# A two-pass channel-attention kernel: first-pass loads in sizes that fall from 44 to 3 rows, and the maxima kept in two halves that take turns

## The chip, the cores and the metric

The kernel runs on one core of one Trainium2 chip. The metric is the device time of one execution in microseconds (us), less is better. Before the change it was 743.05 us (median of 3 runs, 742.87 to 743.95). A "row" in this text is a slice of the input that puts 384 bf16 channels on each of 128 partitions, 98,304 bytes.

## The reference

```python
def reference(x, w1, w2):            # x (1,384,384,384) bf16, w1 (384,96), w2 (96,384)
    xf = x.reshape(B, H * W, C)
    gap = jnp.mean(xf, 1)            # mean over 147,456 pixels, per channel
    gmp = jnp.amax(xf, 1)            # maximum over them
    h_a = relu(gap @ w1)             # (written there as h * (h > 0))
    h_m = relu(gmp @ w1)
    scale = sigmoid(h_a @ w2 + h_m @ w2)
    return x * scale[:, None, None, :]
```

Every output depends on all of x, so x (113.2 MB, 1152 rows) must be read once for the statistics and multiplied afterwards. What stays on chip need not be read again.

## The kernel before

Six slots of 44 rows in SBUF take turns as buffers. In the first pass TensorE adds up each load (sums over partitions with a vector of ones) and VectorE folds it into `acc`, a running maximum over 11 rows. The last 6 x 44 rows stay in the slots, 18 more in PSUM; the other rows are read again in the second pass, where VectorE multiplies slot by slot in place and the ACT queue stores. Between the passes lies the **turn**: `acc` is folded from 11 rows to one, transposed, put through the two small matrices and the sigmoid. No store can start before that, and there is nearly no free memory to load into.

```python
LAST_LOADS = ((22, 22),) * 9 + (      # how the last 14 blocks of 44 rows are cut into loads
    (11, 11, 11, 11), (17, 16, 11), (11, 11, 11, 11), (11, 11, 11, 11), (10, 9, 9, 8, 8),
)
SUM_TAIL = 2                          # loads whose sums take a shorter path at the end
...
for i, (first, n, s, lo, hi) in enumerate(loads):
    rows = slots[s][:, lo:hi, :]
    m = hi - lo
    ...nc.sync.dma_start(out=rows[:, a:b, :], in_=...)
    ...sums(rows, m, ...) or tail_sums(rows, m, ...)            # TensorE
    for j in range(0 if i else A, m, A):                        # A = 11
        k = min(A, m - j)
        nc.vector.tensor_tensor(out=acc[:, 0:k, :], in0=acc[:, 0:k, :], in1=rows[:, j:j + k, :], op=ALU.max)
...
n = A                                                           # the fold: 11 -> 6 -> 3 -> 2 -> 1 rows
while n > 1:
    h = n // 2
    nc.vector.tensor_tensor(out=acc[:, 0:h, :], in0=acc[:, 0:h, :], in1=acc[:, n - h:n, :], op=ALU.max)
    n -= h
    ...                                                         # freed rows of acc are read in again
```

## Time and profile before

| what | value | view |
|---|---|---|
| span of the profiled execution | 741.5 us | page |
| read from HBM, written | 198.92 MB, 113.25 MB | page |
| mean rate | 421 GB/s | page |
| VectorE (DVE) busy | 66% of the span, over 90% in most of the first pass | page |
| fold starts, first multiply | 271.43 us, 276.93 us | chain |

The page cuts the span into 40 slices of 18.5 us. A digit is the busy share in tenths; the last line is what the DMA engines moved:

```profile
DVE  6789999999999989999444443444444444444600
DMA  9999999999999969999999999999999999999997
GB/s 383 423 435 434 433 430 418 428 429 426 427 422 422 418 254 378 402 435 446 432 431 428 432 437 436 436 432 432 427 434 437 436 436 432 432 427 432 441 437 340
```

The DMA engines are full in every slice but the fifteenth, the turn, where they move 254 GB/s (and the last, where the work runs out). VectorE is nearly full from the fourth slice to the fourteenth, but that does not make it the bound: it has about as much work as the loads give it time for.

The table of stretches gives the turn more closely. The columns are the stretch and its length, then busy time and count for TensorE, weight loads, DVE, ACT and POOL, the granted clock, the DMA share and GB/s:

```profile
260.00:270.00 10.00, 6.76 (x75) 3.77 (x70) 9.83 (x6) 0.95 (x4) 0.00 (x0) 0.50 0.81 331
270.00:280.00 10.00, 2.28 (x30) 1.48 (x27) 7.88 (x13) 0.83 (x3) 0.00 (x0) 0.50 0.59 177
280.00:290.00 10.00, 0.00 (x0) 0.00 (x0) 10.00 (x8) 0.00 (x0) 0.00 (x0) 0.50 0.99 396
```

Lost DMA time here is 10 x (1 - 0.81) + 10 x (1 - 0.59), about 6 us. (A packet is counted in the stretch in which it starts, so a share can come out a little over 1.)

TensorE waits for every load in the first pass, so its timeline shows when loads land. The columns are start, busy time, engine, line, operation, and in brackets the idle time before and what ended it:

```profile
25.44 4.06 PE L143 MATMUL bank_a<-x_84,small 128*1 128x512 bf16 x33 [7.40 <-DMA x_84<-in_x_dram]
35.46 4.17 PE L143 MATMUL bank_a<-x_79,small 128*1 128x512 bf16 x33 [5.96 <-DMA x_79<-in_x_dram]
46.95 4.86 PE L143 MATMUL bank_a<-x_80,small 128*1 128x512 bf16 x33 [7.32 <-DMA x_80<-in_x_dram]
...
256.64 1.34 PE L143 MATMUL bank_a<-x_83,small 128*1 128x512 bf16 x9 [1.22 <-DMA x_83<-in_x_dram]
259.22 1.34 PE L143 MATMUL bank_a<-x_83,small 128*1 128x512 bf16 x9 [1.24 <-DMA x_83<-in_x_dram]
```

A 44-row load lands every 10.02 us (35.46 from 25.44), an 11-row load every 2.58 us (259.22 from 256.64; 2.57 on average). The step from 35.46 to 46.95 is 1.5 us too long. From the two sizes, (10.02 - 2.57) / 33 rows makes 0.226 us of DMA time per row. Four loads of 11 rows take about 0.26 us longer than one of 44, which is 0.08 to 0.09 us for each further transfer; the prediction works with 0.083.

The groups by form, those of one slot, give VectorE's cost of a maximum over 11, 10 and 8 rows (4224, 3840 and 3072 elements per partition; busy us and mean ns of one are after the bar, then idle time before them):

```profile
L183 DVE TENSOR_TENSOR acc<-acc,x_84 128x4224 bf16<-128x4224 bf16 x16 | 37.7, 2358 | 5.2 <-DMA x_84<-in_x_dram 4.7
L183 DVE TENSOR_TENSOR acc<-acc,x_84 128x3840 bf16<-128x3840 bf16 x1 | 2.2, 2159 | 0.0
L183 DVE TENSOR_TENSOR acc<-acc,x_84 128x3072 bf16<-128x3072 bf16 x2 | 3.5, 1758 | 0.1
```

Last, the chain of work that ended last, around the turn (start, duration, what):

```profile
267.84 1.77 DVE acc L183
269.61 0.02 issue
269.64 1.77 DVE acc L183
271.40 0.02 issue
271.43 1.17 DVE acc L203
...
276.93 1.50 DVE x_79 L226 x3
```

The maximum of the last 8 rows (269.64 to 271.41) is the last thing before the fold at 271.43. From there to the first multiply it is 5.5 us.

### The profile page before, as it was taken

What the parts mean: (1) busy time and instruction counts of PE and PEld (TensorE: products, weight loads), DVE (VectorE), ACT (ScalarE), POOL (GpSimd) and SP (SyncE); (2) the same over time, 40 slices, a digit from 0 to 9 for tenths busy, and PEclk for the clock granted to TensorE, in tenths of its full rate; (3) what the DMA queues carried; (4) which work ended last, traced back from release to release, by engine and by line L of the source; (5) the groups of instructions that cost most, each with busy time, mean ns of one, the idle gap of its engine ahead of it and who ended that gap; (6) DMA issues with size and microseconds to landing.
All of it is one profiled execution on the core that took longest, in us unless ns stands there. A gap on an engine that the chain in (4) does not pass through costs nothing.

```text
span 741.5 us, 2477 instructions
## 1 busy us (share of the span) xinstructions
PE 127.2 (17%) x966; PEld 40.6 (5%) x966; DVE 489.4 (66%) x168; ACT 3.3 (0%) x9; POOL 0.7 (0%) x6
## 2 busy tenths in 40 slices
PE   3345443445454550000000000000000000000000
PEld 0011111111111120000000000000000000000000
DVE  6789999999999989999444443444444444444600
ACT  0000000000000000000000000000000000000000
POOL 0000000000000000000000000000000000000000
PEclk9865666655555555555555555555555555555555
DMA  9999999999999969999999999999999999999997
GB/s 383 423 435 434 433 430 418 428 429 426 427 422 422 418 254 378 402 435 446 432 431 428 432 437 436 436 432 432 427 434 437 436 436 432 432 427 432 441 437 340
DMA packets 18379, 312.32 MB, mean 421 GB/s; under 512 B 2400, under 2 KB 3008, under 8 KB 6592
## 3 DMA queue, kind: packets, MB, share of 16 engines
q1 hardware_dynamic: 12032, 198.92, 63.2%
q10 hardware_dynamic: 6336, 113.25, 35.7%
q8 instruction: 7, 0.11, 0.1%
q14 instruction: 4, 0.03, 0.0%
HBM read 198.92 MB, written 113.25 MB: 421 GB/s over the span
## 4 chain that ended last, share of the span: by engine, by line
another core or an unknown queue 44%; DMA 34%; DVE 14%; DVEq 1%; SPq 1%; issue 1%; PE 0%; ACT 0%; ACTq 0%
DMA x_81<-in_x_dram 9%; DMA x_82<-in_x_dram 7%; DVE acc L183 7%; DMA out_dram<-x_83 6%; DMA x_79<-in_x_dram 6%; DMA x_80<-in_x_dram 3%; DMA x_83<-in_x_dram 3%; DVE x_81 L226 1%; DVE x_80 L226 1%; DVE x_83 L226 1%; DVE x_82 L226 1%; DVE x_79 L226 1%; DVEq L313 1%; SPq L253 1%
## 5 line engine op out<-in xcount | busy, mean ns | idle before, releaser
L226 DVE TENSOR_TENSOR x_79<-x_79,scale_bc 128x16896 bf16<-128x16896 bf16 (+6 forms) x13 | 45.4, 3538 | 34.2 <-DMA x_79<-in_x_dram 33.0
L226 DVE TENSOR_TENSOR x_80<-x_80,scale_bc 128x16896 bf16<-128x16896 bf16 (+4 forms) x9 | 40.9, 4576 | 28.7 <-DMA x_80<-in_x_dram 28.7
L226 DVE TENSOR_TENSOR x_84<-x_84,scale_bc 128x16896 bf16<-128x16896 bf16 x4 | 35.8, 8958 | 33.1 <-DMA x_84<-in_x_dram 33.1
L226 DVE TENSOR_TENSOR x_83<-x_83,scale_bc 128x16896 bf16<-128x16896 bf16 x4 | 35.8, 8956 | 33.0 <-DMA x_83<-in_x_dram 33.0
L226 DVE TENSOR_TENSOR x_82<-x_82,scale_bc 128x16896 bf16<-128x16896 bf16 x4 | 35.8, 8957 | 32.8 <-DMA x_82<-in_x_dram 32.8
L226 DVE TENSOR_TENSOR x_81<-x_81,scale_bc 128x16896 bf16<-128x16896 bf16 (+3 forms) x6 | 36.0, 6021 | 31.0 <-DMA x_81<-in_x_dram 31.0
L183 DVE TENSOR_TENSOR acc<-acc,x_84 128x4224 bf16<-128x4224 bf16 (+3 forms) x21 | 47.3, 2253 | 5.4 <-DMA x_84<-in_x_dram 4.7
L143 PEld LDWEIGHTS <-small 128*1 128x1 bf16 x900 | 36.4, 110 | 229.9 <-issue 227.0
L183 DVE TENSOR_TENSOR acc<-acc,x_83 128x4224 bf16<-128x4224 bf16 (+1 forms) x19 | 42.8, 2253 | 1.3 <-DMA x_83<-in_x_dram 0.7
L183 DVE TENSOR_TENSOR acc<-acc,x_80 128x4224 bf16<-128x4224 bf16 (+1 forms) x18 | 40.6, 2257 | 3.0 <-DMA x_80<-in_x_dram 2.4
L183 DVE TENSOR_TENSOR acc<-acc,x_79 128x4224 bf16<-128x4224 bf16 (+1 forms) x17 | 38.9, 2287 | 1.5 <-DMA x_79<-in_x_dram 1.0
L183 DVE TENSOR_TENSOR acc<-acc,x_81 128x4224 bf16<-128x4224 bf16 (+2 forms) x17 | 37.9, 2229 | 1.5 <-DMA x_81<-in_x_dram 1.0
L183 DVE TENSOR_TENSOR acc<-acc,x_82 128x4224 bf16<-128x4224 bf16 x16 | 37.7, 2358 | 1.5 <-DMA x_82<-in_x_dram 1.0
L143 PE MATMUL bank_a<-x_84,small 128*1 128x512 bf16 (+2 forms) x165 | 21.6, 558 | 27.1 <-DMA x_84<-in_x_dram 27.1
L143 PE MATMUL bank_a<-x_79,small 128*1 128x512 bf16 (+1 forms) x150 | 20.4, 574 | 28.7 <-DMA x_79<-in_x_dram 28.7
L143 PE MATMUL bank_a<-x_80,small 128*1 128x512 bf16 (+3 forms) x150 | 21.0, 585 | 23.6 <-DMA x_80<-in_x_dram 23.6
L143 PE MATMUL bank_a<-x_83,small 128*1 128x512 bf16 (+2 forms) x159 | 20.3, 540 | 23.3 <-DMA x_83<-in_x_dram 23.3
L143 PE MATMUL bank_a<-x_82,small 128*1 128x512 bf16 (+2 forms) x138 | 19.6, 594 | 20.9 <-DMA x_82<-in_x_dram 20.9
L143 PE MATMUL bank_a<-x_81,small 128*1 128x512 bf16 (+3 forms) x138 | 19.4, 593 | 21.1 <-DMA x_81<-in_x_dram 21.1
L179 DVE COPY acc<-x_79 128x4224 bf16<-128x4224 bf16 x1 | 1.3, 1260 | 5.4 <-DMA x_79<-in_x_dram 5.4
L185 DVE COPY kept_ps<-x_79 128x3072 uint32<-128x3072 uint32 x1 | 3.4, 3354 | 0.0
L226 DVE TENSOR_TENSOR x_81<-kept_ps,scale_bc 128x6144 bf16<-128x6144 bf16 x1 | 3.4, 3350 | 0.0
(39 smaller groups left out, 22.5 us busy)
## 6 DMA issues: line engine op xcount, KB each, us to landing
x_84<-in_x_dram SPq DMA_DIRECT2D x5, 4224.0 KB, 27.4
x_79<-in_x_dram SPq DMA_DIRECT2D x5, 4224.0 KB, 27.4
x_80<-in_x_dram SPq DMA_DIRECT2D x5, 4224.0 KB, 27.7
x_81<-in_x_dram SPq DMA_DIRECT2D x5, 4224.0 KB, 27.4
x_82<-in_x_dram SPq DMA_DIRECT2D x5, 4224.0 KB, 27.4
x_83<-in_x_dram SPq DMA_DIRECT2D x4, 4224.0 KB, 27.4
out_dram<-x_82 ACTq DMA_DIRECT2D x4, 4224.0 KB, 74.3
out_dram<-x_83 ACTq DMA_DIRECT2D x4, 4224.0 KB, 71.1
```

The source lines that it names most:

```text
L143: nc.tensor.matmul(sum_ps[q * QP:q * QP + 1, 0:g * P], lhsT=ones_bf[:, 0:1], rhs=rows[:, k:k + g, q * P:(q + 1) * P], start=(done + k == 0 ...
L179: nc.vector.tensor_copy(out=acc, in_=rows[:, 0:A, :])
L183: nc.vector.tensor_tensor(out=acc[:, 0:k, :], in0=acc[:, 0:k, :], in1=rows[:, j:j + k, :], op=ALU.max)
L185: nc.vector.tensor_copy(out=kept_ps.bitcast(U32), in_=rows.bitcast(U32))
L226: nc.vector.tensor_tensor(out=dst, in0=src, in1=scale_bc.unsqueeze(1).to_broadcast([P, n, C]), op=ALU.mult)
L253: nc.sync.dma_start(out=slots[s][:, j:j + m, :], in_=rows_of(xr, first, n)[:, j:j + m, :])
L313: with _tile.TileContext(nc) as tc:
```

## The change

The intent is to leave less work behind the last byte: the last load has 3 rows instead of 8, and sizes fall, by and large, all the way (within most staying slots they fall once more), so that VectorE, which is only a little faster than the DMA engines, is done with one load when the next lands. Small loads mean small maxima, and each maximum over `acc` used to wait for the one before. So `acc` is used as two halves of 6 and 5 rows in turn, and an operation depends on the one two back.

```diff
+ACC_PARTS = ((0, 6), (6, 11))
-LAST_LOADS = ((22, 22),) * 9 + (
-    (11, 11, 11, 11), (17, 16, 11), (11, 11, 11, 11), (11, 11, 11, 11), (10, 9, 9, 8, 8),
+PASSING = (
+    43, 44, 44, 43, 43, 44, 43, 42, 42, 39, 38, 37, 36, 36, 35, 34, 32, 29, 29, 27, 27, 23, 21, 15, 13,
+)
+STAYING = (
+    (19, 17, 8), (18, 16, 10), (16, 14, 14), (13, 11, 11, 9), (10, 9, 9, 8, 8), (6, 6, 5, 5, 5, 4, 4, 3, 3, 3),
 )
-SUM_TAIL = 2
+SUM_TAIL = 4
...                                   # (building the list of loads from these; the same rows stay and are re-read)
-        for j in range(0 if i else A, m, A):
-            k = min(A, m - j)
-            nc.vector.tensor_tensor(out=acc[:, 0:k, :], in0=acc[:, 0:k, :], in1=rows[:, j:j + k, :], op=ALU.max)
+        j = 0 if i else A
+        while j < m:
+            c, e = ACC_PARTS[turn]
+            turn = (turn + 1) % len(ACC_PARTS)
+            e = min(e, c + m - j)
+            nc.vector.tensor_tensor(
+                out=acc[:, c:e, :], in0=acc[:, c:e, :], in1=rows[:, j:j + e - c, :], op=ALU.max
+            )
+            j += e - c
```

PASSING are the loads of rows that are read again later, STAYING those of the six slots that stay.

More of the change, by code (lines that the diff above doesn't have):

```diff
@@ L71 @@
     head = PSUM_ROWS + beside
-    left = TOT - head
-    blocks = []
-    slot = NS - 1
-    while left > 0:
-        n = min(SLOTS[slot], left)
-        blocks.insert(0, [left - n + head, n, slot])
-        left -= n
-        slot = (slot - 1) % NS
-    n_blocks = len(blocks)
-    n_stream = n_blocks - NS
+    n_stay = sum(SLOTS)
+    n_pass = TOT - head - n_stay
+    assert sum(PASSING) == n_pass
+    stay = []
+    for i, n in enumerate(SLOTS):
+        stay.append([head + n_pass + sum(SLOTS[:i]), n, i])
+    again = [(head, n_pass % SLOTS[0])] + [
+        (head + n_pass % SLOTS[0] + SLOTS[0] * i, SLOTS[0]) for i in range(n_pass // SLOTS[0])
+    ]
     small = consts.tile([P, 16], BF16)
@@ L128 @@
     loads = [(0, PSUM_ROWS, 0, 0, PSUM_ROWS), (PSUM_ROWS, beside, 1, 0, beside)]
-    for i, (first, n, s) in enumerate(blocks):
-        left = n
-        for m in LAST_LOADS[i - n_blocks] if i >= n_blocks - len(LAST_LOADS) else (n,):
-            m = min(m, left)
-            loads.append((first, n, s, n - left, n - left + m))
-            left -= m
-        assert left == 0
+    done = head
+    for i, n in enumerate(PASSING):
+        loads.append((done, n, (i - len(PASSING)) % NS, 0, n))
+        done += n
+    for (first, n, s), pieces in zip(stay, STAYING):
+        assert sum(pieces) == n
+        for j, m in enumerate(pieces):
+            loads.append((first, n, s, sum(pieces[:j]), sum(pieces[:j + 1])))
     n_loads = len(loads)
@@ L163, in tail_sums @@
                 )
-    done = 0
+    done = turn = 0
     for i, (first, n, s, lo, hi) in enumerate(loads):
@@ L254, in get @@
         assert j == 0
-    order = blocks[n_stream:]
-    again = sorted(blocks[:n_stream], key=lambda b: -b[1])
+    order = list(stay)
+    again.sort(key=lambda b: -b[1])
     stores, reads = list(FIRST_STORES), list(FIRST_READS)
@@ L265, in read_into @@
             again.remove(b)
-            b = (b[0], b[1], s)
+            b = (*b, s)
             get(b, reads.pop(0) if reads else (b[1],))
```

## The prediction

> **What bounds the kernel.** Both passes are bound by the DMA engines, not VectorE. The page's slices show DMA at nine tenths or more in every slice but the turn between the passes (254 GB/s); HBM reads 198.92 MB and writes 113.25 MB at a mean 421 GB/s. The change moves no bytes: rows kept on chip and rows re-read stay the same. From the stretch table, DMA idles for about 6 us around the turn (267 to 281 us). That hole is nearly all that the change can win; 2% would be 15 us.
>
> **First pass.** In the timeline TensorE's waits give the landings: a 44-row load every 10.03 us, two of 22 rows every 10.11, four of 11 every 10.27. So a row costs about 0.226 us and each further DMA about 0.083 us (128 packets over 16 engines: about 10 ns per packet; the Trainium skill, "DMA: Bandwidth & Descriptors", Measured, has about 10.5, and the trace agrees). The built programs have 53 first-pass loads before and 56 after: an estimated +0.25 us to the last landing. The six slots and the eight DMA semaphores leave over 6 us of queued loads throughout, so I expect no starvation.
>
> **VectorE.** A maximum over 11 rows takes 2359 ns and starts every 2.39 us, since each waits for the one before. The forms of 3072 and 3840 elements (1758 and 2159 ns) give 0.2 us per row, so a dependent operation has about 190 ns of overhead. Independent multiplies overlap: five on the second staying slot take 9.23 us although their durations sum to 9.56, about 70 ns of overhead each. In the built program each half waits for the operation two back. So 11 rows should cost 2.2 + 2 x 0.07 = 2.34 us: twice the instructions, yet no slower. The halves' worth is that small loads get affordable: one undivided chain needs 0.79 us for 3 rows, against 0.76 between landings.
>
> **The critical part.** Before, the last 8-row load lands at about 269.6 us; its maximum runs 269.64 to 271.4, then fold (2.7 us), transposes, small products, sigmoid, first multiply at 276.9. After, the last load has 3 rows: 0.76 us of maximum behind a landing at about 269.85, so the fold starts at about 270.65. Everything behind it is unchanged. Gain: 1.0 us less behind the last landing, minus 0.25 us of DMA: about 0.75 us. The sums chain (four tail loads, 13 rows instead of 16) stays off the path, ending over 2 us before it is needed. The second pass is the same program shifted. Predicted 742.3 us, 80% range 741.0 to 743.8; faster by over 2% 0.01, within 2% 0.97, slower 0.02.
>
> **What would show it.** Right: maxima of 6 and 5 rows at about 1.36 and 1.16 us but starting 1.27 and 1.07 us apart; a last maximum of 0.76 us that waited for its load; fold 0.5 to 1.2 us earlier; the turn's slice a little fuller, later slices equal. Wrong: VectorE no longer waiting for loads over the last 40 us (it lags), or a last landing over 1 us later.
>
> **What could make it wrong.** Alternating operations may not overlap: then the 3-to-6-row loads leave VectorE behind and the kernel loses about 2 us. About 120 more VectorE instructions mean a few more instruction fetches on the same DMA engines. One 1.5 us landing slip near 44 us, which I cannot explain, may move or vanish. Small descriptors may cost more than 10 ns each.

## The result, and the profile after

The changed kernel took 742.53 us (median of 4 runs, 741.81 to 745.11) against 743.02 (median of 4) before. The ratio is 0.9996 with a 95% interval of 0.9979 to 1.0013. That is inside the predicted range, and by itself it shows no gain: the interval holds both the predicted gain of 0.75 us and zero. The profiled execution was the slowest of the four, 745.11 us.

The slices of the page:

```profile
DVE  5889999999999989998444433434444444433600
DMA  9999999999999979999999999999999999999997
GB/s 381 436 427 432 432 428 431 424 424 438 417 426 420 414 256 376 427 433 433 433 429 435 435 429 433 433 435 435 429 429 429 435 433 436 435 435 427 425 435 310
```

The turn's slice rose from 254 to 256 GB/s only, but the stretches (columns as before) show that the work has moved forward:

```profile
260.00:270.00 10.00, 6.90 (x63) 3.49 (x60) 10.00 (x13) 0.95 (x4) 0.00 (x0) 0.50 0.84 325
270.00:280.00 10.00, 2.44 (x36) 1.64 (x33) 7.88 (x14) 0.83 (x3) 0.00 (x0) 0.50 0.64 194
280.00:290.00 10.00, 0.00 (x0) 0.00 (x0) 10.00 (x9) 0.00 (x0) 0.00 (x0) 0.50 1.02 409
```

From 260 to 270 us the DMA share is 0.84 instead of 0.81, from 270 to 280 it is 0.64 instead of 0.59. By the same sum as before, 10 x (1 - 0.84) + 10 x (1 - 0.64), 5.2 us of DMA time are lost instead of 6.

The groups by form for the halves of 6 and 5 rows (2304 and 1920 elements):

```profile
L190 DVE TENSOR_TENSOR acc<-acc,x 128x2304 bf16<-128x2304 bf16 x95 | 128.5, 1352 | 11.4 <-DMA x<-in_x_dram 11.2
L190 DVE TENSOR_TENSOR acc<-acc,x 128x1920 bf16<-128x1920 bf16 x93 | 106.3, 1151 | 1.4 <-DMA x<-in_x_dram 1.4
```

One operation still takes 1352 and 1151 ns, but they overlap. The timelines of VectorE for one 44-row load show it; first the kernel before, then the changed one:

```profile
47.00 9.54 DVE L183 TENSOR_TENSOR acc<-acc,x_80 128x4224 bf16<-128x4224 bf16 x4 [1.96 <-DMA x_80<-in_x_dram]
```

```profile
29.95 9.44 DVE L190 TENSOR_TENSOR acc<-acc,x 128x2304 bf16<-128x2304 bf16 x8 [0.79 <-DMA x<-in_x_dram]
```

Eight operations in turn take 9.44 us where four in a chain took 9.54. In this load a half of 6 rows starts 1.27 us before the next half, and one of 5 rows 1.07 us.

The chain around the turn:

```profile
267.77 0.68 DVE acc L190
268.65 0.55 DVE acc L190
269.31 0.61 DVE acc L190
269.98 0.76 DVE acc L190
270.75 0.02 issue
270.77 1.17 DVE acc L213
...
276.26 0.83 DVE x L236 x2
```

The fold starts at 270.77 instead of 271.43, and the first multiply at 276.26 instead of 276.93: 0.66 and 0.67 us earlier. The last four maxima start 0.88, 0.66 and 0.67 us apart.

So the turn gained what was forecast, and yet this execution was slower than any of the kernel before in that comparison. Where did it go? The packet records of the trace show two parts. The first 120 MB had moved 0.67 us sooner than in the trace of before (290.30 against 290.97 us after the start of the first load packet), 310 MB at the same moment (731.98 and 731.97), so 0.7 us were lost on the way. The rest was lost at the very end. The DMA share there, in stretches of 1 us, in this execution:

```profile
738.00:739.00 1.00, 0.00 (x0) 0.00 (x0) 0.00 (x0) 0.00 (x0) 0.00 (x0) 0.50 0.30 115
739.00:740.00 1.00, 0.00 (x0) 0.00 (x0) 0.00 (x0) 0.00 (x0) 0.00 (x0) 0.50 0.09 37
740.00:741.00 1.00, 0.00 (x0) 0.00 (x0) 0.00 (x0) 0.00 (x0) 0.00 (x0) 0.50 0.06 25
741.00:742.00 1.00, 0.00 (x0) 0.00 (x0) 0.00 (x0) 0.00 (x0) 0.00 (x0) 0.50 0.06 25
```

A share of 0.06 is one engine of 16 (1/16 = 0.0625). For about 3 us a single engine or two finish the last stores while the others have nothing left. In the second trace of the same program (the first experiment below) the same end is:

```profile
737.00:738.00 1.00, 0.00 (x0) 0.00 (x0) 0.00 (x0) 0.00 (x0) 0.00 (x0) 0.50 0.47 177
738.00:739.00 1.00, 0.00 (x0) 0.00 (x0) 0.00 (x0) 0.00 (x0) 0.00 (x0) 0.50 0.03 11
```

There the engines finish almost together. This end differs from execution to execution, and by more than the gain.

### The profile page after: what moved, and what is told of

Its sections match the earlier page's. It is cut to its first block, busy times and chain, and to the rows that moved or that the text cites. A ratio compares the mean times of both kernels' runs of the same rounds, so it can differ in the third digit from the quotient of the medians.

```text
span 743.3 us, 2595 instructions
## 1 busy us (share of the span) xinstructions
PE 131.4 (18%) x969; PEld 41.7 (6%) x969; DVE 490.1 (66%) x285; ACT 3.3 (0%) x9; POOL 0.7 (0%) x6
## 4 chain that ended last, share of the span: by engine, by line
another core or an unknown queue 40%; DMA 37%; DVE 15%; DVEq 1%; SPq 1%; issue 1%; PE 0%; ACT 0%; ACTq 0%
DMA x<-in_x_dram 31%; DVE acc L190 11%; DMA out_dram<-x 7%; DVE x L236 2%; DVEq L323 1%; SPq L263 1%; DVE kept_ps L195 0%; DVE acc L213 0%; DVE acc L236 0%; DVE acc L183 0%; PE bank_a L230 0%; ACT scale_bc L231 0%; SPq L174 0%; DVE bank_b L197 0%
## 5 line engine op out<-in xcount | busy, mean ns | idle before, releaser
L236 DVE TENSOR_TENSOR x<-x,scale_bc 128x16896 bf16<-128x16896 bf16 (+11 forms) x40 | 229.1, 5769 | 196.4 <-DMA x<-in_x_dram 195.2
L190 DVE TENSOR_TENSOR acc<-acc,x 128x2304 bf16<-128x2304 bf16 (+5 forms) x225 | 245.9, 1166 | 12.8 <-DMA x<-in_x_dram 12.6
L147 PE MATMUL bank_a<-x,small 128*1 128x512 bf16 (+3 forms) x912 | 126.6, 584 | 140.7 <-DMA x<-in_x_dram 140.7
L195 DVE COPY kept_ps<-x 128x3072 uint32<-128x3072 uint32 x1 | 3.4, 3354 | 0.0
L236 DVE TENSOR_TENSOR x<-kept_ps,scale_bc 128x6144 bf16<-128x6144 bf16 x1 | 3.4, 3351 | 0.0
L213 DVE TENSOR_TENSOR acc<-acc 128x384 bf16<-128x384 bf16 (+2 forms) x4 | 2.6, 658 | 0.1
L236 DVE TENSOR_TENSOR acc<-acc,scale_bc 128x1920 bf16<-128x1920 bf16 (+1 forms) x2 | 2.4, 1250 | 0.0
```

The source lines that it names most:

```text
L147: nc.tensor.matmul(sum_ps[q * QP:q * QP + 1, 0:g * P], lhsT=ones_bf[:, 0:1], rhs=rows[:, k:k + g, q * P:(q + 1) * P], start=(done + k == 0 ...
L190: nc.vector.tensor_tensor(out=acc[:, c:e, :], in0=acc[:, c:e, :], in1=rows[:, j:j + e - c, :], op=ALU.max)
L195: nc.vector.tensor_copy(out=kept_ps.bitcast(U32), in_=rows.bitcast(U32))
L236: nc.vector.tensor_tensor(out=dst, in0=src, in1=scale_bc.unsqueeze(1).to_broadcast([P, n, C]), op=ALU.mult)
```

## The experiments

Two numbers are read from every trace. The first is the start of the fold. As executions start up to 0.3 us apart, it is also given from the first landing (marked by the first matmul of the trace). The second is the total over 5 rounds (4 in the first comparison), beside runs of the kernel before on the same chip.

| run | fold, us | from first landing | median, us | before, same rounds | ratio (95%) |
|---|---|---|---|---|---|
| before, first trace | 271.43 | 267.01 | 743.05 | | |
| e1, before again | 271.13 | 266.99 | 743.07 | 742.86 | 1.0003 (0.9989 to 1.0016) |
| changed, first trace | 270.77 | 266.43 | 742.53 | 743.02 | 0.9996 (0.9979 to 1.0013) |
| a1, changed again | 270.45 | 266.24 | 741.24 | 742.25 | 0.9982 (0.9970 to 0.9995) |
| d1, changed a third time | 270.77 | 266.34 | 741.56 | 742.94 | 0.9986 (0.9974 to 0.9999) |
| a2, old sizes, halves | 271.37 | 267.24 | 743.59 | 742.25 | 1.0014 (1.0001 to 1.0026) |
| d3, the same again | 271.65 | 267.32 | 744.22 | 742.94 | 1.0015 (1.0003 to 1.0027) |
| a3, new sizes, one chain | 273.32 | 269.19 | 744.84 | 742.25 | 1.0032 (1.0019 to 1.0044) |
| a4, coarse end | 271.09 | 266.97 | 743.40 | 742.25 | 1.0011 (0.9997 to 1.0024) |
| b1, thrice the loads | 275.90 | 271.59 | 747.54 | 742.50 | 1.0067 (1.0054 to 1.0080) |
| b2, ten more behind | 270.26 | 266.16 | 746.06 | 742.50 | 1.0048 (1.0036 to 1.0060) |
| b3, three more behind | 270.37 | 266.21 | 742.84 | 742.50 | 1.0009 (0.9993 to 1.0024) |
| c1, fewer loads | 270.25 | 266.05 | 742.71 | 742.50 | 1.0006 (0.9991 to 1.0021) |
| d2, fewer loads again | 270.19 | 266.04 | 742.28 | 742.94 | 0.9996 (0.9982 to 1.0009) |

The fold counted from the first landing repeats within 0.03 us for the kernel before (two traces) and within 0.2 us for the changed one (three). The programs of b2 and b3 are the changed kernel up to the fold; with them five traces lie within 0.27 us, so differences of 0.1 to 0.2 us between single traces mean little. The total cannot tell less than about 1 us: the null run e1 has an interval of plus or minus 0.13%. All kernels gave a correct result.

The moment of the last landing can be read too, from the records of the semaphores that the transfers raise (no view above prints them). The fold is then the sum of two parts: when the last rows land, counted from the first matmul, and the time from there to the fold.

| traces | last landing, us | from there to the fold, us |
|---|---|---|
| before, e1 | 265.07, 265.08 | 1.94, 1.90 |
| changed, a1, d1 | 265.54, 265.33, 265.45 | 0.89, 0.91, 0.89 |
| b2, b3 (the same up to the fold) | 265.27, 265.33 | 0.89, 0.88 |
| a2, d3: old sizes, halves | 265.29, 265.37 | 1.96, 1.96 |
| a3: new sizes, one chain | 265.34 | 3.85 |
| a4: coarse end | 265.01 | 1.96 |
| b1: thrice the loads | 270.70 | 0.89 |
| c1, d2: fewer loads | 264.83, 264.81 | 1.22, 1.22 |

In these traces the first maximum over a load never starts less than 0.09 us after the load has landed. One that starts 0.09 or 0.10 us behind therefore waited for its load, and a longer delay means that VectorE came late.

### a1 and d1: the changed kernel again

No edit.

> The changed kernel once more, for a second trace and a tighter interval. My theory (the gain is 1.0 us less work behind the last landing minus 0.25 us of added transfers; the second pass is untouched) expects the fold again at about 270.8 us (270.77 in its first trace, 271.43 before), the first multiply near 276.3, and 742.0 to 742.7 us, 0.3 to 1.0 us under the kernel before of the same rounds; the 2 to 3 us that the first trace lost between 550 and 700 us are chance and should be gone. Rival: the loss late in the second pass belongs to the change, then this trace shows it again and the time is 744 to 745.

> The changed kernel a third time, for pooling. [...] My theory: fold at 270.4 to 270.8 us in this trace too, the first 120 MB moved 0.6 to 1.0 us sooner than before, and the median time 0.3 to 1.3 us under the kernel before of the same rounds. Rival (the first comparison, ratio 0.9996, was the truth and the second, 0.9982, luck): median within 0.3 us of before or above it.

The fold came at 270.45 and 270.77 us. The loss of the first trace did not come back (by the packets it lay on the way to 310 MB and at the end, not between 550 and 700 us as the first text says), and the times were 741.24 and 741.56 us, 1.0 and 1.4 us under the medians of the kernel before. So the rival (the loss belongs to the change) fell, and so did d1's (the first comparison was the truth). The intervals of a1 and d1 hold 0.66 us, the gain at the turn, so the totals do not show more than that; both traces also ended more evenly than those of before. In d1's trace the first 120 MB had moved 0.4 and 0.6 us sooner than in the two traces of before, at or below the low end of what I wrote.

### e1: the kernel before as a null run

No edit.

> The kernel before, submitted as if it were a candidate: a null run, for a second trace of it and for the size of a difference that means nothing. My theory (the 0.7 to 0.9 us at the turn are the change's, the uneven end of the DMA engines is chance): fold at 271.2 to 271.6 us again, the first 120 MB 290.3 to 290.6 us after the first load packet, and a ratio to itself of 0.999 to 1.001. If this trace has the fold at 270.8 or earlier, the gain that I read from one trace of before was chance; if the ratio to itself is 1.001 or more, the 1.0014 of the old sizes with halves means nothing either.

Its fold at 271.13 us is just outside what I wrote, but the trace started earlier: from the first landing it is 266.99 against 267.01. The ratio of the kernel to itself is 1.0003. So the earlier fold of the changed kernel is not chance: 266.99 and 267.01 against 266.43, 266.24 and 266.34, a gain of 0.66 us between the means.

### a2 and d3: the halves alone

```diff
 (the kernel before, its LAST_LOADS and SUM_TAIL)
+ACC_PARTS = ((0, 6), (6, 11))
-for j in range(0 if i else A, m, A): ...            # one chain over 11 rows
+while j < m: c, e = ACC_PARTS[turn] ...             # as in the change
```

> Load sizes of before, maxima in halves of 6 and 5 rows. My theory: the halves alone gain nothing, as the last load still has 8 rows and VectorE was waiting for it before too; fold at 271.4 to 271.6 us, time equal to before within 0.3 us; VectorE only idles more between loads (about 4 us more in the first pass). Rival (VectorE's speed is what the change buys): fold 0.7 us or more earlier than before, time 742.3 or less.

> Old sizes with halves again: its first showing was 743.59 with a fold at 271.37, equal to before's 271.43. If the excess of 0.9 us in the total was only the uneven end of the DMA engines, the median is now within 0.7 us of before; if the halves cost something in the second pass, it is 0.9 us or more over it again.

The fold did not come earlier: 267.24 and 267.32 us from the first landing, 0.2 to 0.3 later than before. All of that is in the last landing, although no transfer was added; I cannot explain it. From there to the fold it is 1.96 us, about as before. So faster maxima alone gain nothing. In total this version is 0.14% slower, twice, about 1 us, where equality within 0.3 us was expected; the fold explains 0.3. The rest I cannot explain: the trace of a2 had moved 310 MB at the same moment as the first trace of before (731.95 and 731.97 us after the start of the first load packet), that of d3 0.6 us later.

### a3: the new sizes alone

```diff
-ACC_PARTS = ((0, 6), (6, 11))
+ACC_PARTS = ((0, 11),)
```

> The new load sizes, maxima over 11 rows in one undivided chain. My theory: a dependent maximum costs about 0.12 us more than one in turn, so VectorE falls behind over the small loads; the fold starts about 2.8 us later than in the changed kernel, at 273.4 to 273.8 us, and the time is about 2.8 us over it, near 745.2. Rival (the sizes alone do it, the halves are decoration): fold at 270.8, time 742.3.

The chain of this kernel at the turn:

```profile
270.95 0.77 DVE acc L190
271.74 0.77 DVE acc L190
272.53 0.77 DVE acc L190
273.32 1.17 DVE acc L213
```

The 3-row maxima start 0.79 us apart here, against 0.66 and 0.67 in the changed kernel: 0.12 us for each operation that waits for the one directly before it. VectorE falls behind: it begins the last slot 2.3 us after that slot's first landing (0.4 in the changed kernel), so most of the delay has built up in the loads before the last slot. The fold comes at 273.32 us, 2.85 us later than in the changed kernel from the first landing (269.19 against 266.34), and the kernel is 0.32% slower than before. The new sizes without the halves are worse than no change.

### a4: the new sizes and halves, but the old end

```diff
-    ..., (10, 9, 9, 8, 8), (6, 6, 5, 5, 5, 4, 4, 3, 3, 3),
+    ..., (10, 9, 9, 8, 8), (10, 9, 9, 8, 8),
-SUM_TAIL = 4
+SUM_TAIL = 2
```

> The changed kernel, but with its last slot loaded as before in 10, 9, 9, 8, 8 rows (two tail loads for the sums, 16 rows). My theory: five loads fewer bring the last landing 0.41 us earlier, but 8 rows of maximum instead of 3 stand behind it (about 1.1 us more), so the fold starts about 0.6 us later than in the changed kernel, at 271.3 to 271.5 us, and the time goes back to that of before, 742.8 to 743.2. Rival (the gain sits in the earlier sizes, 44 to 13 rows): fold at 270.8 or earlier and 742.3 or less.

The fold is back at 266.97 us from the first landing, the value of before. The last landing is 0.4 us earlier than the mean of the changed kernel, and 1.07 us more lie behind it, as computed. So the whole gain at the turn sits in the last slot's sizes. What the finer sizes of the 1108 rows before it are worth is not shown: with the old sizes and halves (a2, d3) VectorE also began the last slot 0.10 us after its first landing, so it came there in time without them. They do need two transfers fewer (46 instead of 48). No run joined the old sizes, the halves and the new last slot. The total, 0.11% over before, is inside what the null run allows. (271.09 us is 0.2 below what I wrote, as this trace started early.)

### b1: what a transfer costs

```diff
+        elif 2 <= i < 2 + len(PASSING):
+            cuts = [0, m // 3, 2 * m // 3, m]       # three transfers for one load, 50 more in all
```

> The changed kernel with each of its 25 passing loads issued as three transfers of a third of the rows: 50 transfers more, same bytes, same maxima. My theory (each transfer costs about 0.083 us of DMA time whatever its size, and the first pass is bound by DMA): the fold starts 50 x 0.083 = 4.1 us later than in the changed kernel, at 274.5 to 275.0 us, and the time is 4 us longer, near 745.5. Rival (the cost I read from loads of 44, 22 and 11 rows is not per transfer): fold within 1 us of the changed kernel's 270.5 to 270.8.

Landings of the same loads near the end, first in the changed kernel, then here:

```profile
264.55 0.70 PE L147 MATMUL bank_a<-x,small 128*1 128x512 bf16 x6 [0.53 <-DMA x<-in_x_dram]
265.75 0.70 PE L147 MATMUL bank_a<-x,small 128*1 128x512 bf16 x6 [0.50 <-DMA x<-in_x_dram]
```

```profile
268.69 0.70 PE L147 MATMUL bank_a<-x,small 128*1 128x512 bf16 x6 [0.51 <-DMA x<-in_x_dram]
270.87 0.70 PE L147 MATMUL bank_a<-x,small 128*1 128x512 bf16 x6 [1.48 <-DMA x<-in_x_dram]
```

From the first landing (4.34 and 4.31 us) the load at 264.55 comes 4.17 us later: (268.69 - 4.31) - (264.55 - 4.34). Divided by 50 that is 0.083 us per transfer, the value used in the prediction. A transfer has 128 packets on 16 engines, so eight packets on each engine take 83 ns, an estimate of 10.4 ns for one. The Trainium skill's page "DMA: Bandwidth & Descriptors", section Measured, has about 10.5 ns per packet, but it divides a floor of 0.67 us by the 64 packets of one small transfer and not by the packets of one engine; counted so, b1 has 0.083 us / 128 = 0.65 ns, and the likeness of the two figures confirms nothing. The next load then slips by another 1 us (2.18 us after the one before, instead of 1.20), which brings the fold to 275.90 instead of the 275.0 expected at most. The total, 747.54 us, is 2 us over the 745.5 expected; this slip is 1 us of that, and the rest is not explained.

### b2 and b3: does the turn pass on one for one?

```diff
+    for _ in range(10):                              # 3 in b3
+        nc.vector.tensor_tensor(out=acc[:, 0:1, :], in0=acc[:, 0:1, :], in1=acc[:, 0:1, :], op=ALU.max)
     for q0, part in tp_ps:                           # the transposes behind the fold
```

> The changed kernel with ten repeated maxima of one row (0.39 us each, idempotent) put behind the fold, before the transposes: 3.9 us of pure chain behind the last landing. My theory: the turn is a hole that the DMA engines cannot fill, so the total grows one for one, by 3.9 us, to about 745.2. Rival (the four runs so far hint at more than the shift of the fold: 2.1 us in total for 0.64 us of fold in the run with the coarse end): growth of 5.5 us or more. Rival (second pass has slack): growth under 2 us.

> The same with three repeated maxima: 1.2 us of chain. One for one: 742.4 to 742.7 us. If a small delay sets the second pass into another, worse rhythm, the time is 743.3 or more, as with the coarse end, and the trace loses the rest after 290 us.

VectorE's timeline in b2, the added operations and the first multiply:

```profile
273.04 3.90 DVE L221 TENSOR_TENSOR acc<-acc 128x384 bf16<-128x384 bf16 x10
279.70 1.49 DVE L238 TENSOR_TENSOR x<-x,scale_bc 128x384 bf16<-128x384 bf16 x3 [1.17 <-ACT scale_bc L233]
```

The first multiply comes at 279.70 us in b2 and at 277.05 in b3, 2.65 us apart. The medians are 3.2 us apart on the same chip (746.06 and 742.84). Against the changed kernel, which ran on another chip, only ratios can be compared: 1.0048 and 1.0009 against 0.9982 and 0.9986, that is 4.6 to 4.9 us for 3.9 us of chain and 1.7 to 2.0 us for 1.2; against the first comparison of the changed kernel (0.9996) it is 3.9 and 1.0. So a delay at the turn is paid in full, with no slack behind it, as the prediction assumed. The steps came out between one for one and 1 us more; that is within the spread of the totals, and I do not claim a factor. b3's 742.84 us lies between what I wrote (742.4 to 742.7) and its rival (743.3 or more). The rival of 5.5 us or more did not come true.

### c1 and d2: a version meant to beat both

```diff
+PASSING = (
+    43, 43, 43, 43, 43, 44, 44, 43, 42, 41, 40, 39, 38, 37, 36, 35, 34, 32, 31, 29, 28, 26, 25,
+)
+STAYING = (
+    (24, 20), (23, 21), (17, 16, 11), (16, 14, 14), (12, 11, 11, 10), (6, 5, 6, 5, 5, 5, 5, 4, 3),
+)
+SUM_TAIL = 3
```

> A version meant to beat both: 49 first-pass transfers instead of 56 (23 passing loads of 43 to 25 rows, staying slots in 24+20, 23+21, 17+16+11, 16+14+14, 12+11+11+10 and 6, 5, 6, 5, 5, 5, 5, 4, 3 rows; three tail loads). Sizes chosen with the measured costs (0.226 us per row and 0.083 per transfer on DMA; 0.2 us per row and 0.07 per maximum on VectorE) so that VectorE just keeps up. My theory: last landing 0.58 us earlier, VectorE ends 0.39 us earlier: fold at 270.1 to 270.4 us, time about 0.4 us under the changed kernel. Rival: VectorE lags, fold at 270.8 or later.

> The version with fewer loads again, beside the changed kernel on one chip. If its 0.4 us earlier fold counts in the total, its median is 0.2 to 0.8 us under the changed kernel's; if its slow first showing (742.71) belongs to it, it is again 0.5 us or more over it though its fold is again at 270.1 to 270.4 us.

The chain of c1 at the turn:

```profile
269.47 0.76 DVE acc L190
270.23 0.02 issue
270.25 1.17 DVE acc L213
```

The first pass is shorter as computed: the last landing comes 0.6 us before the changed kernel's mean, but VectorE is 0.3 us late there (1.22 us to the fold instead of 0.89). The fold is at 266.05 and 266.04 us from the first landing, 0.3 us before the changed kernel's 266.34 (0.4 expected). It does not show in the total: 742.71 and 742.28 us, with single runs from 741.43 to 745.43. In the second showing it ran beside the changed kernel and was 0.7 us slower by medians. I do not call it better; the changed kernel stays the fastest by its totals.

### The uneven end, counted

The packet records allow one more reading: how long before the end the last moment with 16 packets in flight lies. It was 2.1 and 2.6 us in the two traces of before, 4.1, 1.1 and 0.8 us in the three of the changed kernel, 2.6 and 2.8 with old sizes and halves, 2.9 and 1.5 with fewer loads. That is a spread of over 3 us between executions, on a kernel whose change is worth 0.7. No run here took it away, so what sets it stays open, and so does whether the changed kernel's two even ends were luck.

## Why the prediction was right

The total, 742.53 us, lies 0.2 us from the predicted 742.3, but with a spread of 1 us that closeness is partly luck. Point by point:

- **DMA bounds both passes, and only the turn's hole can be won.** Right. b2 and b3 show that a delay at the turn is paid in full, and b1 that a longer first pass is too.
- **0.083 us per transfer, so 0.25 us for three more.** Right in its rate: b1 measured 0.083 over 50 transfers. The last landing itself came 0.20 to 0.47 us later than before, 0.31 in the mean of five traces. Three transfers need not be the whole cause of that: a2 and d3, with no more transfers than before, landed 0.2 and 0.3 us later too.
- **1.0 us less behind the last landing.** Right: 1.94 and 1.90 us before, 0.88 to 0.91 in five traces. This and the landing make up the gain at the fold: 1.03 - 0.31 = 0.72 us in the mean of the five (0.66 with the three traces of the changed kernel alone).
- **Halves: 2.34 us for 11 rows instead of 2.39.** Right: the halves start 1.27 and 1.07 us apart, 2.34 together, and 44 rows take 9.44 us against 9.54.
- **The halves' worth is that small loads get affordable, about 2 us lost without them.** Right: a3 came 2.2 us later than before at the fold (269.19 against 267.00) and 0.32% (2.4 us) slower in total.
- **Fold at about 270.65, gain about 0.75 us.** Right: 270.77, and a gain of 0.66 us between the means of the traces.
- **A last maximum that waited for its load; VectorE no longer waiting over the last 40 us would be a bad sign.** Right, and nearly at the limit. The last maximum began 0.11, 0.13 and 0.11 us after its load had landed (changed, a1, d1), where 0.09 is the least ever seen. The two before it began about 0.24 and 0.17 us after theirs: VectorE was a little late and caught up, as its maxima started 0.66 and 0.67 us apart and the loads landed 0.72 to 0.75 apart. In each of the three traces 8 or 9 of the 22 loads that landed after 231 us were waited for. The table of waits has only 0.2 us of this, as it lists longer idle times alone; read by itself it would have looked like the bad sign.
- **Later slices equal.** Right on the average, but the prediction treated the second pass as a constant. It is a constant only within about 1 us, and its end within 3.

## What to carry to other kernels

What a stage boundary costs is the work behind the last landing, so make the last loads small, but only after making the operations on them cheap: without the halves the same sizes lost 2 us (a3; it shows this for all the new sizes together, not for the last slot alone). Choose the sizes by two measured lines, one for the transfer (0.226 us per row and 0.083 per transfer here) and one for the operation (0.2 us per row and 0.07 per operation), so that the slower engine is done when the next load lands. When the expected gain is a tenth of a per cent, judge it at the stage by a mark in the trace, counted from a start mark, and run the kernel against itself before believing a total.

## What the Trainium skill lacked or had wrong

- "VectorE: DVE Perf Modes", section The DRAIN you can't avoid: it reports that eight copies took the same time with a semaphore after each and with one at the end, so that the semaphore costs nothing extra. That does not carry over from copies to in-place maxima, where each reads what the one before it wrote: 3-row operations that wait for the one directly before start 0.79 us apart (a3), those that wait for the one two back 0.66 to 0.67 (changed kernel). The section gives no figure for a wait on the operation two back.
- "DMA: Bandwidth & Descriptors", section Measured: its figure of about 10.5 ns per packet is for one small transfer issued from GpSimd, counted over all 64 packets of it. It does not say what one more transfer costs in a full stream issued from the SP queue: 0.083 us for 128 packets on 16 engines (b1).
- No page read says how unevenly the 16 engines finish after a long stream: the last stores drained for 0.8 to 4.1 us after the last moment with 16 packets in flight.
- No page read says what an instruction fetch does to a stream of loads. In the traces of the changed kernel and of before, one landing is 1.3 to 1.5 us late (the step from 35.46 to 46.95 us before), and the DMA part of the page has one 16 KB instruction fetch between 30 and 42 us, in that step. b1's second slip, 1 us at 270.87, also has a fetch (8 KB, between 267 and 272 us). Most other fetches show no slip (two show 0.3 and 0.5 us), and no run tested this: it is a coincidence seen several times, not a shown cause.
